# Reordering the halves of the first MLP over three blocks, and taking the first expert pairs' weight splits off GpSimd, in a fused attention–MLP–MoE kernel

## Chip, cores and metric

One NeuronCore of a Trainium2 chip runs the whole program in one launch. The metric is the device time of that launch in microseconds; a kernel's figure is the median of its runs. A chance or a verdict "within 0.2%" means within about 2.2 us.

## What is computed

Three stages follow one another, all in float32. Windowed attention (4 sequences of 768 tokens, 8 heads of 64, chunks of 32 queries that see 16 keys to the left, 8 to the right and 8 memory keys) gives 3072 rows of 512. A dense MLP and then a mixture of 8 experts follow:

```
x = attention(q, k, v, mem_k, mem_v)                  # 3072 x 512
h = x @ w_in                                          # 512 x 2048
g = h * tanh(softplus(h))
y = g @ w_out                                         # 2048 x 512
logits = normalise(y) @ normalise(expert_emb).T / tau
e, p = argmax(logits), softmax(logits)[argmax]
out = p * (relu(y @ w1[e]) @ w2[e])                   # w1[e] 512 x 1024, w2[e] 1024 x 512
```

To keep float32 accuracy each operand of the large products is split into a high and a low part of TensorE's float32 format, and three products are taken: high by high, high by low, low by high.

## The kernel before

**Attention** is cut into 48 sub-units of 64 queries, six to a block of 384 tokens, eight blocks. A sub-unit takes transposes of q and k (`T`), scores (`S`), a softmax on VectorE and ScalarE whose division `norm` (line 453) runs on VectorE or GpSimd, the transposes of the probabilities (`PT`), the product with v (`V`), and the split of the result into `xt`, the block's MLP input (1.5 MB, high and low parts). There are two `xt` buffers.

**The first MLP** has 128 steps. Step s works on one block j and one slice f of 128 of the 2048 hidden units. On TensorE it has `H`, twelve matmuls into `p_h` (line 539), and `Y`, nine matmuls into three accumulators `p_y` (line 585). Between them ScalarE and VectorE evaluate the activation: tanh, square, exp (ScalarE), `m` (line 558), square (line 562, ScalarE), `rr` (line 565), `g` (line 568), `gh` and `gl` (line 576). `p_h` has two buffers, so `H` of step s needs the `g` of step s-2, which is the last reader of its buffer. The accumulators have one buffer each.

The first time that a slice of w_in or w_out is used its 32 pieces must have been loaded (`raw`) and split (`sign`, `high`, `low`, `hi`, `lo`: lines 286 to 316, most of it on VectorE). So the program's front has three streams on VectorE at once: attention, pieces of weights, and the activation. To spread the pieces, before runs the slices of block 0 in two halves: (block 0, slices 0–7), (block 1, slices 0–15), (block 0, slices 8–15), then blocks 2 to 7 in full. The partial y of block 0's first half is evacuated (`out0`), stored in DRAM (`y_p`) and added later.

**Routing** computes the logits of each tile of 128 tokens as the MLP ends it, and then, in two groups (21 tiles, last 3 tiles), the expert of each token and its place: a chain of some dozens of small VectorE operations per group (lines 796 to 1035).

**The experts** run in units of 256 tokens of one expert (pairs) or 128 (singles). The first three pairs, u = 0, 1, 2, come from group 1 alone, and lie at the end of the MLP and beside the routing of group 2. Each pair gathers two tiles of rows (`xg`, an indirect DMA issued by GpSimd), transposes them (`xT`), and loads eight 512 KB chunks of w1 and w2 (`eraw`). Each chunk is split: `ehi` is a copy (ScalarE or VectorE, line 246 is the copy helper) and `elo` a subtraction (VectorE or GpSimd, line 1163). TensorE then runs `eH`, matmuls into `p_h` (line 1191), the relu halves `hh` follow on VectorE (lines 1202, 1208), and `eY`, matmuls into `p_y` (line 1281). The result is scattered to the output by GpSimd (`out_dram`).

**What sets the order.** All instructions are ordered by a planner (`Plan.order`). Each job has a rank and a planned duration on each engine that may do it; the planner simulates the engines, gives each job to the engine that ends it first, and emits the jobs in that order. The order of each engine's queue is then fixed; the chip only waits on the semaphores. Operations in the set `PORT` (line 87) are planned as if VectorE and GpSimd could not run them at the same time as GpSimd's own; the small routing operations (`r`, `ids`) are not in that set. A matmul group of another kind behind the last costs `SWITCH` in the plan.

The lines that set the MLP's order, and the engines of the experts' splits:

```
order = ([(0, f) for f in range(HALF)] + [(1, f) for f in range(KFF)] + [(0, f) for f in range(HALF, KFF)]
         + [(j, f) for j in range(2, NBLK) for f in range(KFF)])
put_job(("shi", u, second, c), hi, {A: 947} if j in (0, 2, 4, 5, 7) else {V_: 602}, ...)
put_job(("slo", u, second, c), lo, {G: 2303} if j in (1, 4, 6) else {V_: 1135}, ...)
```

Of the kernel before, what the change touches and what calls it, by code (L numbers as in the profile page):

```python
# [85 lines left out]

PORT = {"sign", "high", "low", "hi", "lo", "rg", "norm", "rn", "m", "rr", "gh", "gl", "yb2", "yb3", "shi", "slo"}


class Plan:  # L90
# [24 lines left out]
    def order(self):  # L115
        end, on, free, todo, waits, tiled, cols, port = {}, {}, {}, {}, {}, False, {}, 0.0
# [79 lines left out]
def attn_moe_moe_kernel(ctx, tc, q, k, v, mem_k, mem_v, w_in, w_out, emb, tau, w1, w2, cst, out, ydbg=None):  # L196
# [71 lines left out]
    def piece(n):  # L268
# [49 lines left out]
        r = 2 * n - 50 if n < 4 else 0.5 * n - (6 if n < NPIECE // 2 else 0)  # L318
# [16 lines left out]
    def attention(u):  # L335
# [3 lines left out]
        R = lambda x: x + (3 * u - 60 if first else 1.4 * u - 16 if u < 2 * SPB else 1.5 * u + 2 if u < 3 * SPB else 8 * u / 3 - 20.4)  # L339
# [148 lines left out]
        job(("T", u), T, {E: 437 if odd else 560}, rank=R(0), after=[("qk", u)], use=[(t, u) for t in qkt] + ([kt] if odd else []),  # L488
# [30 lines left out]
    y_p = dram.tile([BLK, DM], F32, name="y_p")  # L519

    def mlp(s):
        j, f = order[s]
        g, o = divmod(f, WG)
        first = f == 0 or (j, f) == (0, HALF)
        final = f == KFF - 1 or (j, f) == (0, HALF - 1)
        new = j == (0 if f < HALF else 1)
        yh = (j, f // HALF if j == 0 else 0)

# [915 lines left out]
```

## Time and profile before

| | before |
|---|---|
| median of 3 runs | 1094.82 us (1093.49 to 1095.75) |
| the profiled execution | 1091.25 us |
| its span, first to last instruction | 1089.5 us |
| mean granted TensorE clock over the span | 0.989 |
| TensorE busy | 1054.7 us (97%) |
| VectorE busy | 784.4 us (72%) |
| ScalarE busy | 685.1 us (63%) |
| GpSimd busy | 187.6 us (17%) |

The profile is one execution, followed by instruction. [...] On a timeline an instruction's duration reaches a little into the next one's, so the cost of one in a full queue is the spacing of the starts.

### The profile page before, as it was taken

The page shows a single profiled execution, that of the slowest core. Times are in us where ns is not written, and L with a number is a line of the kernel's source. Part 1 is how long each engine was busy: PE and PEld are TensorE (multiplying, and loading weights), DVE is VectorE, ACT ScalarE, POOL GpSimd, SP SyncE. Part 2 cuts the span into 40 slices and gives each one's busy share as a digit, 9 for nine tenths or more (in the row PEclk, how much of TensorE's full clock was granted, in tenths as well). Part 3 has the DMA queues.
Part 4 walks back from the last instruction along what each step waited for, and adds up shares of the span by engine and source line. Part 5 has one row for each costly group of instructions (what it writes and reads, how often), then busy time and mean ns, then how long its engine had stood idle before and what let it go on. Part 6 is the DMA issues. An engine that isn't in the chain of part 4 may idle for free. (4 is left out here: it accounts for less than half of the span.)

```text
span 1089.5 us, 20349 instructions
## 1 busy us (share of the span) xinstructions
PE 1054.7 (97%) x7501; PEld 923.2 (85%) x7501; DVE 784.4 (72%) x1611; ACT 685.1 (63%) x1559; POOL 187.6 (17%) x114
## 2 busy tenths in 40 slices
PE   8898999999999999999999999999989999999996
PEld 6687888888888888888888889888889889998995
DVE  4999996667676576567667566797995558777851
ACT  4787887667777777768777777855424334444441
POOL 0000000000000000000000000014455545665542
PEclk9999999999999999999999999999999999999998
DMA  7954411322112112112112100019349768568200
GB/s 185 285 169 124 138 30 32 77 69 66 28 43 60 37 38 57 35 36 66 37 30 67 25 14 30 1 41 386 145 160 400 254 233 259 200 205 273 86 31 21
DMA packets 154767, 121.81 MB, mean 112 GB/s; under 512 B 98010, under 2 KB 127066, under 8 KB 154660
## 3 DMA queue, kind: packets, MB, share of 16 engines
q1 hardware_dynamic: 150340, 107.06, 32.2%
q0 software_dynamic: 4320, 13.37, 3.4%
q8 instruction: 61, 1.00, 0.4%
q14 instruction: 46, 0.38, 0.1%
HBM read 115.43 MB, written 14.16 MB: 119 GB/s over the span
## 5 line engine op out<-in xcount | busy, mean ns | idle before, releaser
L539 PE MATMUL p_h<-xt,win_h 128*128 128x384 f32 x1024 | 271.8, 347 | 6.0 <-DVE rn L568 5.9
L539 PEld LDWEIGHTS p_h<-xt,win_h 128*128 128x128 f32 x1024 | 182.4, 189 | 14.8 <-DVE rn L568 5.8
L539 PE MATMUL p_h<-xt,win_l 128*128 128x384 f32 x512 | 173.5, 339 | 0.4 <-DVE win_l L316 0.4
L585 PE MATMUL p_y<-wout_h,gh 128*128 128x512 f32 x384 | 155.1, 404 | 0.5 <-ACT gh L246 0.5
L585 PE MATMUL p_y<-wout_h,gl 128*128 128x512 f32 x384 | 152.1, 396 | 0.6 <-DVE gl L576 0.6
L585 PE MATMUL p_y<-wout_l,gh 128*128 128x512 f32 x384 | 151.6, 395 | 0.0
L1281 PE MATMUL p_y<-ehi,hh 128*128 128x512 f32 x432 | 142.1, 398 | 0.4 <-DVE hh L1250 0.4
L246 ACT CAST ehi<-eraw 128x1024 fp32r<-128x1024 f32 x80 | 83.7, 1049 | 90.7 <-PE p_y L1281 54.7
L1163 DVE TENSOR_TENSOR elo<-eraw,ehi 128x1024 fp32r<-128x1024 f32 x80 | 113.8, 1428 | 34.9 <-ACT ehi L246 34.7
L1163 POOL TENSOR_TENSOR elo<-eraw,ehi 128x1024 fp32r<-128x1024 f32 x48 | 119.4, 2488 | 110.0 <-ACT ehi L246 53.7
L1191 PE MATMUL p_h<-xs,ehi 128*128 128x256 f32 x704 | 131.4, 288 | 5.9 <-DVE hh L1208 2.2
L558 DVE SCALAR_TENSOR_TENSOR m<-sq,rn 128x384 f32<-128x384 f32 x128 | 71.0, 555 | 84.1 <-ACT rn L236 83.4
L1191 PEld LDWEIGHTS p_h<-xs,ehi 128*128 128x128 f32 x704 | 111.9, 193 | 9.0 <-ACT ehi L246 3.3
L543 ACT ACTIVATE sq<-p_h 128x384 f32<-128x384 f32 x128 | 61.8, 483 | 69.2 <-PE p_h L539 69.2
L562 ACT ACTIVATE m<-m,c 128x384 f32<-128x384 f32 x128 | 78.7, 615 | 39.5 <-DVE m L558 38.8
L1191 PE MATMUL p_h<-xs,elo 128*128 128x256 f32 x352 | 100.8, 286 | 1.0 <-DVE elo L1163 1.0
L539 PEld LDWEIGHTS p_h<-xt,win_l 128*128 128x128 f32 x512 | 96.7, 189 | 0.8 <-DVE win_l L316 0.8
L1281 PEld LDWEIGHTS p_y<-ehi,hh 128*128 128x128 f32 x432 | 81.2, 188 | 18.8 <-DVE hh L1250 1.3
L585 PEld LDWEIGHTS p_y<-wout_h,gl 128*128 128x128 f32 x384 | 72.3, 188 | 18.4 <-DVE gl L576 1.0
L565 DVE SCALAR_TENSOR_TENSOR rn<-m,rn 128x384 f32<-128x384 f32 x128 | 71.4, 558 | 20.7 <-ACT m L562 20.0
L1281 PE MATMUL p_y<-elo,hh 128*128 128x512 f32 x216 | 85.2, 394 | 0.0
L585 PEld LDWEIGHTS p_y<-wout_h,gh 128*128 128x128 f32 x384 | 72.4, 189 | 13.6 <-ACT gh L246 0.7
(261 smaller groups left out, 1884.1 us busy)
## 6 DMA issues: line engine op xcount, KB each, us to landing
eraw<-in_moe_w_dram SPq DMA_DIRECT2D x128, 512.0 KB
raw<-in_moe_w_in_dram SPq DMA_DIRECT2D x16, 512.0 KB
raw<-in_moe_w_out_dram SPq DMA_DIRECT2D x16, 512.0 KB
y_d<-ysb SPq DMA_DIRECT2D x24, 256.0 KB
qn<-in_q_dram SPq DMA_DIRECT2D x43, 128.0 KB
kn<-in_k_dram SPq DMA_DIRECT2D x35, 128.0 KB
vn<-in_v_dram SPq DMA_DIRECT2D x20, 176.0 KB
vn<-in_v_dram SPq DMA_DIRECT2D x20, 128.0 KB
```

The source lines that it names most:

```text
L246: (nc.scalar.copy if e == A else nc.vector.tensor_copy)(out, src)
L539: nc.tensor.matmul(p, w, xt[j][:, a, kk, :], start=(n == 0), stop=(n == len(ops) - 1))
L543: nc.scalar.activation(t, tl["h", s], AF.Tanh, scale=0.5)
L558: nc.vector.scalar_tensor_tensor(t, tl["sq", s], 4.0, tl["rn", s], ALU.add, ALU.mult)
L562: nc.scalar.activation(t, t, AF.Square, bias=c15)
L565: nc.vector.scalar_tensor_tensor(tl["rn", s], tl["m", s], 0.75, tl["rn", s], ALU.add, ALU.mult)
L585: nc.tensor.matmul(yp[yh][t], x[:, c], w[g][:, o, :], start=(first and n == 0), stop=(final and n == 2))
L1163: engs[e].tensor_sub(tl["elo", j], raw[b, second, c], tl["ehi", j].bitcast(F32))
L1191: nc.tensor.matmul(p[:, o, :], w[:, kk, s], v[:, kk, :], start=(kk == 0 and m == 0), stop=(kk == KDM - 1 and m == 2))
L1281: nc.tensor.matmul(tl["yy", u][a], v[:, kk, s], w[:, k, :], start=(kk == 0 and m == 0), stop=(kk == KEF - 1 and m == 2))
```

## The change

It has three parts.

1. **MLP order** (`LEAVE = 2`). The first halves of three blocks come first, then their second halves: (block 0, slices 0–7), (block 1, 0–7), (block 2, 0–15), (block 1, 8–15), (block 0, 8–15), then blocks 3 to 7. The second half of the weights is first used at step 24 instead of 16, and its pieces' rank is moved by 5 steps. The attention of blocks 1, 2 and 3 gets other ranks. Three blocks are now under way with two `xt` buffers, so block 0's `xt` is stored in DRAM (`x_p`) after step 7 and read back after step 31 by a DMA on GpSimd's queue; `V` of unit 12, the first writer of block 2's `xt`, takes the buffer that the store frees. Block 1's partial y is now stored and added too, as block 0's was.
2. **Splits of the first three pairs.** All `ehi` of u < 3 go to ScalarE, and all `elo` to VectorE. Per pair that moves three `elo` from GpSimd to VectorE and three `ehi` from VectorE to ScalarE.
3. **Planner.** `r` and `ids` join `PORT`, the switch cost depends on the two kinds of matmul (`between`), a few planned durations change, and gathers are kept in order.

```diff
+LEAVE = 2
+DENSE = {"mm_h", "mm_y", "H", "Y"}
+def between(a, b):
+    if a in DENSE:
+        return 92 if b in ("T", "S", "yL") else 0
+    if b in DENSE:
+        return 0 if a is None else 20 if a in ("PT", "yT", "xT", "hT") else 90
+    return 93 if a in ("PT", "yT") and b in ("T", "S") else 0
-PORT = {"sign", "high", "low", "hi", "lo", "rg", "norm", "rn", "m", "rr", "gh", "gl", "yb2", "yb3", "shi", "slo"}
+PORT = {"sign", "high", "low", "hi", "lo", "rg", "norm", "rn", "m", "rr", "gh", "gl", "yb2", "yb3", "shi", "slo", "r", "ids"}
...
-        r = 2 * n - 50 if n < 4 else 0.5 * n - (6 if n < NPIECE // 2 else 0)
+        r = 2 * n - 50 if n < 4 else 0.5 * n - 6 if n < NPIECE // 2 else 0.5 * n + 5
...
-        R = lambda x: x + (3 * u - 60 if first else 1.4 * u - 16 if u < 2 * SPB else 1.5 * u + 2 if u < 3 * SPB else 8 * u / 3 - 20.4)
+        R = lambda x: x + (3 * u - 60 if first else 1.4 * u - 16 if u < (LEAVE + 1) * SPB else 2 * o + 32 if j == LEAVE + 1 else 8 * u / 3 - 20.4)
...
-    order = ([(0, f) for f in range(HALF)] + [(1, f) for f in range(KFF)] + [(0, f) for f in range(HALF, KFF)]
-             + [(j, f) for j in range(2, NBLK) for f in range(KFF)])
+    order = ([(j, f) for j in range(LEAVE) for f in range(HALF)] + [(LEAVE, f) for f in range(KFF)]
+             + [(j, f) for j in reversed(range(LEAVE)) for f in range(HALF, KFF)]
+             + [(j, f) for j in range(LEAVE + 1, NBLK) for f in range(KFF)])
...
+    def x_away():
+        def store(e):
+            nc.sync.dma_start(out=x_p.bitcast(F32), in_=flat_x(xt[0]).bitcast(F32))
+        def load(e):
+            xt[0] = xp.tile([128, 2, KDM, BLK], F32R, tag="xt", name="xt")
+            nc.gpsimd.dma_start(out=flat_x(xt[0]), in_=x_p)
+        s0, s1 = at[0, HALF - 1], at[LEAVE, KFF - 1]
+        plan.dma(("xstore",), store, dict(SP=470), 3 * 2 ** 19, s0, [("mm_h", s0)], use=[("xt", 0)])
+        plan.dma(("xload",), load, dict(Pool=1100), 3 * 2 ** 19, s1, [("mm_h", s1), ("xstore",)], get=[("xt", ("xt", 0, 1))])
...
-            put_job(("shi", u, second, c), hi, {A: 947} if j in (0, 2, 4, 5, 7) else {V_: 602}, rk, [("ld", u, second, c)], [(f"w{16 + 2 * j}", h1)], [hr_])
-            put_job(("slo", u, second, c), lo, {G: 2303} if j in (1, 4, 6) else {V_: 1135}, rk, [("shi", u, second, c)], [(f"w{17 + 2 * j}", h2)], [hr_, h1])
+            put_job(("shi", u, second, c), hi, {A: 947} if j in (0, 2, 4, 5, 7) or u < FIRST // 2 else {V_: 602}, rk, [("ld", u, second, c)] + ([("shi", u - 1, second, c)] if u else []), [(f"w{16 + 2 * j}", h1)], [hr_])
+            put_job(("slo", u, second, c), lo, {G: 2303} if j in (1, 4, 6) and u >= FIRST // 2 else {V_: 1135}, rk, [("shi", u, second, c)], [(f"w{17 + 2 * j}", h2)], [hr_, h1])
```

What this does to the queues is shown at three places. Line numbers are those of each kernel: GpSimd's `elo` is line 1163 before and 1197 after, the gathers 1086 and 1119, the scatters 1307 and 1341.

GpSimd's queue from the end of the MLP over the first pairs, before:

```order
L1086 DMA xg<-y_d,gi 128x512 x2
L975 CAST ei<-ef 1x3
L1086 DMA xg<-y_d,gi 128x512 x2
L1163 TENSOR_TENSOR elo<-eraw,ehi 128x1024 x5
L1086 DMA xg<-y_d,gi 128x512 x2
L1163 TENSOR_TENSOR elo<-eraw,ehi 128x1024
L1307 DMA out_dram<-yo,si 3072x512 x2
L1163 TENSOR_TENSOR elo<-eraw,ehi 128x1024 x2
L1086 DMA xg<-y_d,gi 128x512 x2
L975 CAST ei<-ef 1x20
L1163 TENSOR_TENSOR elo<-eraw,ehi 128x1024
```

The same place after:

```order
L1119 DMA xg<-y_d,gi 128x512 x2
L1007 CAST ei<-ef 1x3
L1119 DMA xg<-y_d,gi 128x512 x4
L1341 DMA out_dram<-yo,si 3072x512 x3
L1119 DMA xg<-y_d,gi 128x512 x2
L1007 CAST ei<-ef 1x20
L1341 DMA out_dram<-yo,si 3072x512
L1197 TENSOR_TENSOR elo<-eraw,ehi 128x1024
```

Nine `elo` stand in this stretch before (5, 1, 2 and 1). After, only DMAs and one cast of 20 numbers are left until the pairs of group 2.

VectorE's queue in the routing of group 2, where it first meets the pairs (`rc`, `ra`, `rh`, `rd`, `o` are routing; `hh` is the relu), before:

```order
L867 TENSOR_TENSOR ra<-ra,rh 128x24
L1208 SCALAR_TENSOR_TENSOR hh<-p_h_9281,hh 128x512
L868 TENSOR_REDUCE rc<-ra 128x3
L246 CAST ehi<-eraw 128x1024
L869 CAST rc<-rc 128x3
L1163 TENSOR_TENSOR elo<-eraw,ehi 128x1024
L870 TENSOR_SCALAR rc<-rc 128x3
L1208 SCALAR_TENSOR_TENSOR hh<-p_h_9326,hh 128x512
L871 TENSOR_SCALAR rc<-rc 128x3
L872 CAST rh<-rc 128x3
```

After:

```order
L899 TENSOR_TENSOR ra<-ra,rh 128x24
L1197 TENSOR_TENSOR elo<-eraw,ehi 128x1024
L900 TENSOR_REDUCE rc<-ra 128x3
L1197 TENSOR_TENSOR elo<-eraw,ehi 128x1024
L901 CAST rc<-rc 128x3
L1242 SCALAR_TENSOR_TENSOR hh<-p_h_9338,hh 128x512
L902 TENSOR_SCALAR rc<-rc 128x3
L1197 TENSOR_TENSOR elo<-eraw,ehi 128x1024
L903 TENSOR_SCALAR rc<-rc 128x3
L1197 TENSOR_TENSOR elo<-eraw,ehi 128x1024
L904 CAST rh<-rc 128x3
```

The copies `ehi` have left VectorE, and more subtractions `elo` stand between the small routing operations.

GpSimd's queue from the program's start to the end of the MLP (`win`, `wout` and `raw` are pieces of weights, `pr` is the attention's division), before:

```order
L240 TENSOR_SCALAR win_h<-sp 128x512
L453 TENSOR_TENSOR pr<-pr,sm 128x384 x4
L576 TENSOR_TENSOR gl<-rn,gh 128x384
L1086 DMA xg<-y_d,gi 128x512 x2
```

After:

```order
L466 TENSOR_TENSOR pr<-pr,sm 128x384
L253 TENSOR_SCALAR win_h<-sp 128x512
L253 TENSOR_SCALAR wout_h<-sp 128x512
L466 TENSOR_TENSOR pr<-pr,sm 128x352
L329 TENSOR_TENSOR win_l<-sp,win_h 128x512
L329 TENSOR_TENSOR wout_l<-sp,wout_h 128x512
L253 TENSOR_SCALAR raw<-raw 128x512
L329 TENSOR_TENSOR win_l<-sp,win_h 128x512
L466 TENSOR_TENSOR pr<-pr,sm 128x384
L543 DMA xt<-x_p 128x3072
L1119 DMA xg<-y_d,gi 128x512 x2
```

Nine elementwise operations now stand ahead of the reading back of `x_p`; before, five stood in the same stretch of the program, and one more at its end.

## Rows read from the trace of the kernel before

**Rows 1.** The page's first part: busy us, share of the span, instructions.

```profile
PE 1054.7 (97%) x7501; PEld 923.2 (85%) x7501; DVE 784.4 (72%) x1611; ACT 685.1 (63%) x1559; POOL 187.6 (17%) x114
```

**Rows 2.** Stretches (start:end, length, busy us and instructions by engine, PEclk, DMA share, GB/s).

```profile
50.00:100.00 50.00, 45.25 (x342) 37.10 (x341) 49.58 (x110) 42.51 (x111) 1.09 (x1) 0.92 0.58 163
100.00:150.00 50.00, 47.48 (x270) 40.51 (x269) 48.43 (x99) 42.11 (x92) 0.00 (x0) 0.98 0.36 113
...
200.00:250.00 50.00, 48.91 (x463) 41.92 (x460) 35.31 (x85) 34.12 (x101) 2.48 (x3) 1.00 0.31 76
...
850.00:1050.00 200.00, 199.59 (x1308) 181.26 (x1308) 141.99 (x148) 88.66 (x113) 111.99 (x65) 1.00 0.59 198
```

**Rows 3.** The same by 10 us where the first expert pairs and group 2's routing lie.

```profile
750.00:760.00 10.00, 9.96 (x69) 9.57 (x69) 8.79 (x19) 4.39 (x5) 5.86 (x3) 0.83 1.06 401
...
800.00:810.00 10.00, 8.57 (x57) 8.40 (x58) 9.96 (x29) 2.25 (x3) 6.03 (x5) 0.83 0.57 163
```

**Rows 4.** TensorE's waits, 690 to 1089 us: who waited for whom, us, times, longest.

```profile
PE p_h L1191 <- DVE hh L1208: 2.2, 1, 2.2
PE p_h L1191 <- DVE rb L806: 1.7, 1, 1.7
PE p_h L539 <- DVE rn L568: 1.2, 1, 1.2
PE p_h L1191 <- DVE xs L1144: 1.0, 1, 1.0
PE p_h L1191 <- DVE elo L1163: 1.0, 1, 1.0
PE p_h L1191 <- ACT ehi L246: 0.8, 1, 0.8
```

**Rows 5.** VectorE's timeline, routing of group 2: start, us, instruction [idle before].

```profile
744.73 2.36 DVE L1163 TENSOR_TENSOR elo<-eraw,ehi 128x1024 fp32r<-128x1024 f32 x2 [2.06 <-ACT ehi L246]
...
762.79 2.33 DVE L871 TENSOR_SCALAR rc<-rc 128x3 int32<-128x3 int32 x1
765.03 0.16 DVE L872 CAST rh<-rc 128x3 bf16<-128x3 int32 x1
...
793.33 1.21 DVE L1163 TENSOR_TENSOR elo<-eraw,ehi 128x1024 fp32r<-128x1024 f32 x1
...
794.54 0.67 DVE L246 CAST ehi<-eraw 128x1024 fp32r<-128x1024 f32 x1
...
803.46 4.30 DVE L1008 TENSOR_TENSOR rhs<-rhs,rb 128x96 bf16<-128x96 bf16 x12
```

**Rows 6.** GpSimd's timeline in the same stretch.

```profile
750.28 4.72 POOL L1163 TENSOR_TENSOR elo<-eraw,ehi 128x1024 fp32r<-128x1024 f32 x2 [7.43 <-DVE lg L681]
...
762.71 2.39 POOL L1163 TENSOR_TENSOR elo<-eraw,ehi 128x1024 fp32r<-128x1024 f32 x1 [0.46 <-ACT ehi L246]
...
803.55 2.40 POOL L1163 TENSOR_TENSOR elo<-eraw,ehi 128x1024 fp32r<-128x1024 f32 x1 [0.63 <-DVE rb L806]
```

**Rows 7.** ScalarE's `ehi`, by line (instruction, count, busy us, mean ns).

```profile
L246 ACT CAST ehi<-eraw 128x1024 fp32r<-128x1024 f32 x80 | 83.7, 1049 | 90.7 <-PE p_y L1281 54.7
```

**Rows 8.** Stretches of 10 us in the front, one of them and the sum.

```profile
sum 120.00, PE 109.49 PEld 92.67 DVE 117.89 ACT 101.05 POOL 1.09; mean PE 9.12 PEld 7.72 DVE 9.82 ACT 8.42 POOL 0.09
```

**Rows 9.** TensorE's waits, 40 to 300 us.

```profile
PE p_h L539 <- DVE rn L568: 4.7, 5, 2.0
```

**Rows 10.** GpSimd's timeline in the front.

```profile
20.68 0.86 POOL L240 TENSOR_SCALAR win_h<-sp 128x512 fp32r<-128x512 f32 x1 [20.22 <-DVE sp L298]
73.88 1.09 POOL L453 TENSOR_TENSOR pr<-pr,sm 128x384 f32<-128x384 f32 x1 [52.34 <-ACT m L562]
...
247.44 0.83 POOL L453 TENSOR_TENSOR pr<-pr,sm 128x384 f32<-128x384 f32 x1 [26.10 <-ACT xt L246]
```

**Rows 11.** VectorE's timeline beside two of these.

```profile
74.19 1.18 DVE L565 SCALAR_TENSOR_TENSOR rn<-m,rn 128x384 f32<-128x384 f32 x1
...
247.77 0.54 DVE L568 SCALAR_TENSOR_TENSOR rn<-rn,p_h 128x384 f32<-128x384 f32 x1
```

More of the change, by code (lines that the diff above doesn't have):

```diff
@@ L115, in order @@
     def order(self):
-        end, on, free, todo, waits, tiled, cols, port = {}, {}, {}, {}, {}, False, {}, 0.0
+        end, on, free, todo, waits, tiled, last, cols, port = {}, {}, {}, {}, {}, False, None, {}, 0.0
         shared = lambda k, e: e == "Pool" and k[0] not in ("gather", "scatter", "issue", "experts") or e == "DVE" and k[0] in PORT
@@ L158, in order @@
                 t = max(t, t0)
-                if tiled > j["tiled"]:
-                    t += SWITCH
-                tiled = j["tiled"]
+                t += between(last, k[0])
+                last, tiled = k[0], j["tiled"]
                 d = self.stream(cols, t, d, SHARE.get(k[0], 1)) - t
@@ L487, in attention @@
         kt = ("kT", pair)
[L488 removed]
+        job(("T", u), T, {E: 560 if odd else 630}, rank=R(0), after=[("qk", u)], use=[(t, u) for t in qkt] + ([kt] if odd else []),
             get=[("a", t1), ("a", t2), ("qT", ("qT", u))] + ([] if odd else [(ktt, kt)]))
@@ L523, in mlp @@
         g, o = divmod(f, WG)
[L524 to L527, printed above, removed]
+        first = f == 0 or j < LEAVE and f == HALF
+        final = f == KFF - 1 or j < LEAVE and f == HALF - 1
+        new = j == (0 if f < HALF else LEAVE)
+        yh = (j, f // HALF if j < LEAVE else 0)
+        X = ("xt", 0, 1) if j == 0 and f >= HALF else ("xt", j)
         htag = "a" if j == NBLK - 1 and f % 3 == 2 else "h"
@@ L610, in rows @@
         j, t = divmod(i, TPB)
-        yh = (j, 1 if j == 0 else 0)
-        half = slice(t * 128, (t + 1) * 128)
+        yh = (j, 1 if j < LEAVE else 0)
+        half = slice(i * 128, (i + 1) * 128)
         def out0(e):
             tl["y0", i] = att.tile([128, DM], F32, tag=tag0, bufs=dict(kT=1, pT=2)[tag0], name="y0")
-            scale(e, tl["y0", i], yp[0, 0][t], 8.0)
+            scale(e, tl["y0", i], yp[j, 0][t], 8.0)
         def store0(e):
@@ L1091, in unit @@
         for a in range(nt):
+            gathers.append(("issue", "gather", u, a))
             put_job(("gather", u, a), gather(a), {G: 1038}, base - 4,
-                    [("places", g)] + [("ystore", i) for i in range(T1 if g == 1 else NTILE)], [("vn", ("xg", u, a))], dma=2 ** 18)
+                    [("places", g)] + gathers[-2:-1] + [("ystore", i) for i in range(T1 if g == 1 else NTILE)], [("vn", ("xg", u, a))], dma=2 ** 18)
         def load(second, c):
```

44 lines of the change are left out of this document (26 added, 18 removed).

## Prediction

> **What bounds the kernel now.** I read the busy times first: TensorE works 1054.7 of 1089.5 us [rows 1], so at most some 35 us can go without less work, and what matters is where TensorE stands still. The table of stretches puts that in four places [rows 2]: 50 to 100 us (4.75 us idle, and a granted clock of 0.92), 100 to 150 (2.52 us, 0.98), 200 to 250 (1.09 us), and the first expert pairs at 700 to 850. From 850 to 1050 TensorE is busy 199.59 of 200 us, so a gain made earlier is not given back there; the tail after 1050 is not touched by the change.
>
> In the front VectorE is the bound: it works 117.89 of the 120 us from 40 to 160 [rows 8], and TensorE's waits there name its activation step `g` (4.7 us in five waits) [rows 9]. That is the stretch in which attention, weight pieces and activation share VectorE.
>
> In the expert stretch the waits of TensorE are 2.2 (for `hh`), 1.7, 1.2, 1.0, 1.0 and 0.8 us, 7.9 us in all, four of the six on VectorE's routing or relu work and one on its `elo` [rows 4]. Twice the granted clock is 0.83 there, at 750 to 760 and 800 to 810, after such waits [rows 3]: a stretch of 10 us at 0.83 loses (1 − 0.83) × 10 = 1.7 us of work each, 3.4 us. Together that is 11.3 us: the ceiling of what the second part of the change can give.
>
> Why VectorE is late there is on two timelines read side by side. A routing step on 128x3 numbers takes 0.16 us at 765.03, but the one at 762.79 takes 2.33 us and ends at 765.12; GpSimd's `elo` of 762.71 took 2.39 us and ended at 765.10 [rows 5, 6]. The twelve small products at 803.46 take 4.30 us beside the `elo` of 803.55 [rows 5, 6]. There are eight such stretched instructions between 751 and 808; each less what its kind takes alone gives 0.8, 2.1, 2.2, 2.2, 2.2, 1.8, 2.0 and 2.3 us, about 15.7 us of VectorE's time lost beside nine `elo`.
>
> **The change, part by part.** *Splits of the first pairs.* It removes nine `elo` from GpSimd and with them the 15.7 us of stretching. It adds nine `elo` to VectorE, whose spacing is 1.14 us (793.33 to 794.47, the 1.21 us less the overlap) [rows 5]: +10.3 us. It takes nine `ehi` from VectorE at 0.60 us spacing (0.67 on the row) [rows 5]: −5.4 us. VectorE's balance is −15.7 + 10.3 − 5.4 = −10.8 us between about 740 and 808, where it is at 9.96 of 10 us in 800 to 810 [rows 3]. ScalarE takes nine copies of 1.05 us [rows 7]: 9.4 us, in stretches where it is busy 4.39 and 2.25 of 10 us [rows 3]; I put them at nothing, covered by that idle time, and if the cover is gone they are the rival below.
>
> What TensorE gets of the 10.8 us goes wait by wait. The 2.2 (`hh`), 1.7 and 1.0 us (`rb`, `xs`) come behind stretched instructions and should go: 4.9 us. The other three, 1.2, 0.8 and 1.0 us, belong to the first pair's start, when chunks arrive and are split and only one `elo` stands on GpSimd; I take a third of their 3.0 us, 1.0. Of the clock I take the whole second loss, 1.7, and most of the first, 1.4, which lies after these start waits. That is 9.0 us. Bounds: 3 us, if only the wait for `hh` and a little clock go, and 11.3 us. I lean to the upper end because VectorE's relief exceeds the sum of the waits that hang on it. What is late next is the chunks' landing: the DMA engines are full at 750 to 760 (401 GB/s) [rows 3], and those loads start no earlier for the first pairs.
>
> *Order of the MLP.* Pieces of the second half may come eight steps later, but attention of blocks 1 and 2 comes earlier instead. I added up the instructions in front of step 22's `H` in each order, each kind at its mean spacing. VectorE has 13.5 us more ahead of it than before (more score additions, maxima, x splits and copies; four fewer piece subtractions), TensorE 13.0 us more. Before, VectorE was 1.8 us ahead of TensorE at that point; by these sums it now binds and TensorE has lost 1.3 us less than it had. So the front stays bound by VectorE and the half order mostly exchanges one kind of work for another: −1.3 us. The idle 1.09 us at 200 to 250 [rows 2], where attention of block 3 and block 0's return lay, I halve: −0.5. The bounds of the front's own gain are 0 and 5 us, the latter if half of the 8.4 us idle in the three stretches and some of the clock's loss go.
>
> The order's price has three terms. Block 0's `xt` is stored, 1.5 MB; at the 401 GB/s that full DMA engines reached [rows 3] that is 3.9 us, at the 163 GB/s of 50 to 100 us [rows 2] 9.6 us. `V` of unit 12 must wait for it and stands some 10 us of TensorE's work after step 7: nothing, or up to about 3 us with what is queued ahead of the store; VectorE, the bound, has other work meanwhile, so a wait under 5 us costs nothing. Behind the store on SP's queue stand loads of q, k, v and pieces, which have no users for several steps. The reading back has eight steps of 4.2 us for the same transfer: nothing. Block 1's partial y adds three evictions, stores and loads, beside TensorE's work: nothing; they fall after VectorE's full stretch.
>
> GpSimd's elementwise work is the third term. Nine operations now stand ahead of the reading back, where two were at work before 200 us. Three divisions at 0.83, three copies-with-scale at 0.86 [rows 10] and three subtractions, half as long as an `elo` (1.2 us, an estimate from the 2.39 of [rows 6]), make 8.7 us, against 0.86 + 1.09 [rows 10] before: 6.7 us more. What that costs VectorE is not one number: beside the division of 73.88 (1.09 us) the step at 74.19 took 1.18 us, 0.63 longer than the 0.55 of its kind, and beside that of 247.44 nothing was longer [rows 10, 11]. The ends are 0 and 6.7 × 0.63 / 1.09 = 3.9 us; I take the middle, +2.0.
>
> [...]
>
> *Planner.* The new costs and `PORT` entries move instructions but add none. I cost them at nothing; the sums above are made from the resulting orders.
>
> **The sum**, against the profiled 1091.25 us: −9.0 − 1.3 − 0.5 + 2.0 = −8.8; 1082.5. That execution lies 3.6 us under the median of the runs shown, and the median is what is forecast: 1094.82 − 8.8 = 1086.0 us.
>
> **The rivals.**
>
> *The front gains as well.* If the added GpSimd work stretches nothing and the front's gain is its upper 5 us, with an expert gain of 9 to 10, the sum is −14 to −15: 1080. For it: VectorE is the front's bound and some of its work has gone to GpSimd. Against it: the work moved in ahead of step 22 weighs as much as what moved out.
>
> [...]
>
> *The expert stretch is bound by its loads.* Then the start waits and the first clock loss remain and only about 3 us go: 1094.8 − 3 − 0.5, about 1091. For it: the DMA engines are full at 750 to 760. Against it: the waits name VectorE, not a DMA.
>
> *Nothing reaches the end.* The stretches go, but as many `elo` now stand ahead of each routing step and relu, so that the chain to the places and to `hh` is no earlier: 1094.8. The order after does show two `elo` more between such steps.
>
> *Slower: VectorE waits for ScalarE.* Each of the moved chunks now needs a ScalarE copy before VectorE's `elo`, and behind that `elo` on VectorE's queue stand the routing steps and `hh`. The row at 744.73 shows such a wait, 2.06 us for an `ehi` [rows 5]. Nine of these are 18.5 us; with −10.8 that is +7.7 on a full VectorE, and −0.5 from the front: 1102. It is no gain from a mean wait of 10.8 / 9 = 1.2 us on, and slower by over 0.2% from about 1.5 us on. For it: ScalarE works in order and the copies queue behind relu halves and x copies. Against it: ScalarE is idle over half of the stretch, and most chunks landed early.
>
> **How the numbers follow.** Forecast 0.50 (1082.5 to 1089.5); the front gains as well 0.12; the port is held 0.08; bound by loads 0.13; nothing reaches the end 0.07; slower 0.10. A difference within 0.2%, about 2.2 us, is what a measurement here can't tell from none. Faster by more: 0.50 + 0.12 + 0.08 + 0.10 of the loads' case = 0.80. Within: the rest of the loads' case and nearly all of "nothing", 0.09. Slower: 0.11. The range 1079.5 to 1092.5 holds the forecast, the port, most of the front's and the loads' cases: 0.80.
>
> **What would show it.** Between 740 and 800 no routing step of VectorE over 1 us, GpSimd without `elo`, TensorE's waits for `hh`, `rb` and `xs` gone, and the clock at 1.00 in the second of the two stretches: right on the pairs. VectorE at over 97% from 40 to 160, now with instructions stretched beside GpSimd's nine, and TensorE's loss by step 22 within 2 us of before: right on the front. A wait of TensorE of over 5 us at `V` of unit 12, or waits of VectorE for `ehi` above 1.2 us in the mean, would make the prediction wrong; so would the last pair's `eY` ending no more than 5 us earlier than before when counted from the last MLP step.

## The result and the profile after

| | before | after |
|---|---|---|
| median, measured together (4 runs each) | 1095.28 us (1093.49 to 1098.51) | 1080.14 us (1078.09 to 1083.69) |
| ratio, 95% interval | | 0.9862 (0.9827 to 0.9897) |
| the profiled execution | 1091.25 us | 1080.64 us |
| its span | 1089.5 us | 1078.8 us |

The change is 15.1 us faster; 1086.0 had been forecast, and the range 1079.5 to 1092.5 holds the time. The two profiled executions lie 10.6 us apart: before's is 4.0 us under its median, after's 0.5 us over. The traces explain the 10.6.

After's busy times, as in [rows 1] (us, share, instructions):

```profile
PE 1050.8 (97%) x7499; PEld 920.4 (85%) x7499; DVE 776.7 (72%) x1605; ACT 694.1 (64%) x1574; POOL 170.1 (16%) x109
```

After's stretches, columns as in [rows 2] (start:end, length, busy of PE, PEld, DVE, ACT, POOL, granted clock as a share of the full one, DMA share, GB/s):

```profile
0.00:50.00 50.00, 42.91 (x490) 34.40 (x490) 36.73 (x87) 30.97 (x106) 1.02 (x5) 1.00 0.84 228
50.00:100.00 50.00, 47.98 (x405) 39.75 (x406) 49.32 (x115) 41.88 (x121) 4.90 (x4) 0.93 0.68 193
100.00:150.00 50.00, 49.89 (x377) 42.52 (x377) 49.60 (x112) 42.32 (x110) 3.26 (x3) 1.00 0.52 150
150.00:200.00 50.00, 47.09 (x267) 41.00 (x266) 39.12 (x101) 39.02 (x91) 1.20 (x1) 1.00 0.14 39
200.00:250.00 50.00, 50.00 (x306) 44.68 (x305) 31.08 (x64) 37.97 (x84) 0.76 (x1) 1.00 0.21 69
...
750.00:800.00 50.00, 50.00 (x346) 45.31 (x345) 47.77 (x157) 28.93 (x39) 11.12 (x9) 1.00 0.49 178
800.00:850.00 50.00, 49.73 (x340) 44.92 (x340) 36.72 (x37) 19.52 (x27) 29.88 (x15) 1.00 1.04 383
850.00:1050.00 200.00, 196.72 (x1276) 177.75 (x1275) 141.15 (x146) 86.92 (x112) 107.30 (x63) 1.00 0.56 182
```

Against [rows 2]: TensorE works 2.7 and 2.4 us more in the two stretches from 50 to 150, and 750 to 850 is almost without a gap. Two places are worse: 150 to 200 has 2.9 us idle where before had none, and 850 to 1050 lost 3.3 us where before lost 0.4. The 2.9 us are three waits: 1.5 for ScalarE's copy `kT` (157.82), 0.8 for `g` (162.56) and 0.6 for a small VectorE step (174.94). TensorE's waits late in the program, as in [rows 4] (690 to 1080 us):

```profile
PE p_y L1315 <- DVE hh L1284: 3.3, 3, 1.2
PE p_yT L674 <- ACT ysb L249: 1.2, 1, 1.2
PE p_y L614 <- DVE gh L259: 0.5, 1, 0.5
PE p_lg L701 <- DVE yt L259: 0.4, 1, 0.4
PE p_h L1225 <- DVE xs L1178: 0.3, 1, 0.3
```

The six waits of [rows 4] are gone from the first pairs: the three on the activation and the chunks at their start have given way to those in the three middle rows (for `ysb`, `gh` and `yt`, 2.1 us), and the 0.3 us for `xs` belong to u = 4. The 3.3 us in the first row lie behind the pairs, in the singles; before has 0.4 us in two waits there, below the rows shown in [rows 4].

**Where the time went.** TensorE does the same work in both kernels, so its lead over before can be read at equal points of the work: the start of the last `H` but one (719.89 before, 714.00 after), the end of `eY` of u = 2 (827.2 and 813.0) and of u = 4 (875.3 and 861.5), and the last matmul's end (1079.3 and 1068.6). The differences of these leads give what each stretch won, 5.9, 8.3, −0.4 and −3.1 us: the front 5.9, the first three pairs 8.3, and 3.5 given back after them. This table is used for all kernels below.

### The profile page after: what moved, and what is told of

The parts are those of the page before. It is cut to its first block, busy times and chain, and to the rows that moved or that the text cites. A ratio compares the mean times of both kernels' runs of the same rounds, so it can differ in the third digit from the quotient of the medians.

```text
span 1078.8 us, 20397 instructions
## 1 busy us (share of the span) xinstructions
PE 1050.8 (97%) x7499; PEld 920.4 (85%) x7499; DVE 776.7 (72%) x1605; ACT 694.1 (64%) x1574; POOL 170.1 (16%) x109
## 3 DMA queue, kind: packets, MB, share of 16 engines
q1 hardware_dynamic: 151348, 110.21, 33.5%
## 5 line engine op out<-in xcount | busy, mean ns | idle before, releaser
L1197 DVE TENSOR_TENSOR elo<-eraw,ehi 128x1024 fp32r<-128x1024 f32 x89 | 133.4, 1507 | 40.8 <-ACT ehi L259 39.0
L259 ACT CAST ehi<-eraw 128x1024 fp32r<-128x1024 f32 x89 | 92.8, 1048 | 100.5 <-PE p_y L1315 51.4
L1119 POOL DMA_INDIRECT xg<-y_d,gi x27 | 29.7, 1100 | 556.1 <-DVE si L1067 507.5
L1197 POOL TENSOR_TENSOR elo<-eraw,ehi 128x1024 fp32r<-128x1024 f32 x39 | 95.0, 2437 | 82.4 <-ACT ehi L259 47.5
```

The source lines that it names most:

```text
L259: (nc.scalar.copy if e == A else nc.vector.tensor_copy)(out, src)
L1119: nc.gpsimd.indirect_dma_start(out=tl["xg", u, a], out_offset=None, in_=y_d[0:T1 * 128, :] if g == 1 else y_d[:, :], in_offset=bass.Indire ...
L1197: engs[e].tensor_sub(tl["elo", j], raw[b, second, c], tl["ehi", j].bitcast(F32))
```

## The experiments

Ratios are to before in the same series, with 95% intervals; the four series had medians of before of 1092.51, 1094.18, 1092.52 and 1091.66 us. After was not measured again in them: its ratio is that of the result above, from four runs of each kernel, and has the widest interval. The names of the parts are those of the diff above: 1 MLP order, 2 splits, 3 planner.

**Each part alone, and each left out.** `splits_only` is before with part 2, `order_only` with part 1, `planner_only` with part 3; `no_splits`, `no_order` and `no_planner` are after without one. Their edits are the lines shown in the diff, put into before or taken back from after; the first and the last as samples:

```diff
 # splits_only, on before
-{A: 947} if j in (0, 2, 4, 5, 7) else {V_: 602}
+{A: 947} if j in (0, 2, 4, 5, 7) or u < FIRST // 2 else {V_: 602}
-{G: 2303} if j in (1, 4, 6) else {V_: 1135}
+{G: 2303} if j in (1, 4, 6) and u >= FIRST // 2 else {V_: 1135}
 # no_planner, on after
-                t += between(last, k[0])
+                if tiled > j["tiled"]:
+                    t += SWITCH
-"shi", "slo", "r", "ids"}
+"shi", "slo"}
```

Expected of `splits_only`: 

> The kernel before with the second part of the change alone: for the first three pairs every ehi on ScalarE and every elo on VectorE; MLP order and planner as before. If the nine GpSimd subtractions cost the pairs' stretch what the two traces show (the lead of the changed kernel grows from 4.8 us at the last MLP step to 14.1 at the third pair's first matmul, so 9.3 there), this run has 1095 - 9 = 1086 us, and no routing step of VectorE over 1 us between 740 and 800. If it is the planner's new entries that clear the stretch, and the splits only move work, it is within 3 us of before.

Expected of `order_only`: 

> The kernel before with the first part of the change alone: first halves of three blocks, then second halves, attention ranks with it, block 0's x stored and read back; splits and planner as before. If the order of the MLP alone makes the front's gain, TensorE reaches the last MLP step 4 to 5 us earlier and the run has 1095 - 5 = 1090 us. If my sum for the front was right (1.3 + 0.5 less 2.0 for GpSimd's added work, about nothing) and the gain of the front comes from the planner's new durations and switch costs, it is 1094 to 1096.

Expected of `planner_only`: 

> The kernel before with the third part alone: r and ids in the set that is planned as excluding GpSimd, the switch cost by kinds, the changed planned durations, gathers in order. Charged at nothing in the prediction: 1093 to 1097 us. If the planner's entries are what clears the routing of stretched steps, 1086 to 1090.

Expected of `no_planner`: 

> The changed kernel without the third part: MLP order and splits as changed, planner as before. The parts alone gave ratios of 0.9914 (splits), 0.9921 (order) and 1.0002 (planner). If splits and order work in different places and add up, 0.9836: about 1075 us, faster than the changed kernel. If the changed kernel's smaller total (0.9862) is the ceiling of what TensorE can be given, whatever the planner, 1078 to 1081.

Expected of `no_splits`: 

> The changed kernel with the first three pairs' splits as before: order and planner changed. The planner alone won 4 to 5 us in the front and lost about 8 in the pairs' stretch, where nine elo were still on GpSimd. If that is what it does with GpSimd's elo, this run repeats it: about 1093 + 0 to -4, 1089 to 1094. If the order and the planner add up without it, 1084.

Expected of `no_order`: 

> The changed kernel with the MLP order of before: splits and planner changed. If order and planner both win the same idle time in the front (each alone reaches the last MLP step earlier than before, the order by about 8 us and the planner by about 5), this run keeps the planner's share and the splits' 9: 1080 to 1083. If only the order wins in the front, 1084 to 1087.

Measured, with the gains by stretch from each trace (us, minus is a loss against before):

| parts | kernel | ratio | front | u = 0–2 | u = 3, 4 | rest |
|---|---|---|---|---|---|---|
| 2 | `splits_only` | 0.9914 (0.9894–0.9933) | 0.4 | 8.3 | 0.1 | −0.7 |
| 1 | `order_only` | 0.9921 (0.9903–0.9938) | 8.0 | −0.3 | 0.0 | −0.4 |
| 3 | `planner_only` | 1.0002 (0.9990–1.0013) | 6.3 | 3.0 | −11.2 | −1.1 |
| 1, 2 | `no_planner` | 0.9838 (0.9822–0.9855) | 8.3 | 8.4 | 0.0 | −4.1 |
| 1, 3 | `no_splits` | 1.0003 (0.9991–1.0016) | 6.6 | 4.1 | −12.7 | −0.1 |
| 2, 3 | `no_order` | 0.9865 (0.9846–0.9884) | 4.8 | 8.3 | 0.1 | −3.8 |
| 1, 2, 3 | after | 0.9862 (0.9827–0.9897) | 5.9 | 8.3 | −0.4 | −3.1 |

Three things follow. Every kernel with the splits has won 8.3 to 8.4 us at the first pairs. Alone, the splits account for all of it; beside part 3 they do not, since 3.0 to 4.1 us are won there without them, and what they then add most is that the 11 to 13 us at u = 3 and 4 are not lost. The order alone gives 8.0 us in the front, which no sum of mine had; but beside part 3 it adds nothing (0.9865 without it, 0.9862 with it), since the planner's new costs win 4.8 to 6.3 us in the front by themselves, and the two gains do not add up (5.9 and 6.6 us with both). And part 3 is not neutral: with `elo` on GpSimd it loses 11 to 13 us at u = 3 and 4, as much as it wins before. Parts 1 and 2 add up as independent gains would: 0.9914 × 0.9921 = 0.9836, measured 0.9838.

In `order_only` the stretches show the front's gain: 45.25 and 47.48 became 46.41 and 50.00 us, and the clock 0.97 and 1.00 where it was 0.92 and 0.98 [rows 2].

```profile
50.00:100.00 50.00, 46.41 (x403) 38.22 (x404) 49.37 (x115) 43.29 (x127) 2.77 (x3) 0.97 0.68 191
100.00:150.00 50.00, 50.00 (x380) 42.96 (x379) 49.50 (x110) 42.97 (x112) 4.17 (x3) 1.00 0.52 154
```

In `planner_only` the loss at u = 4 stands on the timelines of VectorE, GpSimd and TensorE:

```profile
831.47 2.37 DVE L1176 TENSOR_TENSOR elo<-eraw,ehi 128x1024 fp32r<-128x1024 f32 x1
833.76 0.69 DVE L257 CAST ehi<-eraw 128x1024 fp32r<-128x1024 f32 x1
834.37 3.79 DVE L1176 TENSOR_TENSOR elo<-eraw,ehi 128x1024 fp32r<-128x1024 f32 x1
838.08 0.68 DVE L1221 SCALAR_TENSOR_TENSOR hh<-p_h,hh 128x512 fp32r<-128x512 f32 x1
838.68 1.27 DVE L1157 TENSOR_TENSOR xs<-p_xT,xs 128x512 fp32r<-128x512 f32 x2
```

```profile
830.38 2.38 POOL L1176 TENSOR_TENSOR elo<-eraw,ehi 128x1024 fp32r<-128x1024 f32 x1 [6.21 <-issue]
...
834.71 2.35 POOL L1176 TENSOR_TENSOR elo<-eraw,ehi 128x1024 fp32r<-128x1024 f32 x1
```

```profile
840.01 0.58 PE L1204 MATMUL p_h<-xs,ehi 128*128 128x256 f32 x1 [5.01 <-DVE xs L1157]
```

Two of VectorE's `elo` take 2.37 and 3.79 us instead of 1.21 [rows 5] beside GpSimd's two, the `xs` queued behind them is 3.7 us late, and TensorE waits 5.0 us for it. That is part of the 11.2 us: in the same stretch TensorE also waits 1.9 us for a GpSimd `elo` itself and 0.7 us twice, and the clock falls once (3.4 us). The group's places, the last step of routing, come at 804.45 us (798.70 before) although the front was 6.3 us earlier. Which of part 3's edits puts these pieces beside one another was not tried; that `r` and `ids` now yield to GpSimd in the plan fits the later routing, and is argued only.

**Is it GpSimd's work that delayed VectorE?** `dummies` gave after GpSimd work again at the first pairs, nine subtractions into a scratch tile, cut into eight pieces each:

```diff
+for n in range(8):
+    z = slice(128 * n, 128 * n + 128)
+    nc.gpsimd.tensor_sub(dummy, raw[b, second, c][:, z], tl["ehi", j][:, z].bitcast(F32))
```

> The changed kernel with nine GpSimd subtractions put back in the first three pairs (each in eight pieces of 128 columns), which read the same chunk and its high part, and write a scratch tile that nobody reads; the order on every other engine is that of the changed kernel, instruction for instruction, and the output is the same. If GpSimd's subtractions hold up VectorE's own instructions, routing steps between 740 and 800 are stretched again, VectorE loses up to the 21 us that nine of them last, and the time is 1080 + 5 to 10 = 1085 to 1090 us. If the stretching before came from something else (the order, waits on data), no step is stretched and the time stays within 2 us of 1080.

It took 1.0040 (1.0024–1.0055), but tells little: the 72 pieces took 51 us, and ScalarE's next `ehi` had to wait for these readers of the old one:

```profile
762.39 1.04 ACT L260 CAST ehi<-eraw 128x1024 fp32r<-128x1024 f32 x1 [7.19 <-POOL dummy L1210]
```

That is another wait than the one in question. VectorE's order is after's, so its instructions can be compared one by one: from 735 to 810 us 34 of them are longer, each by 0.2 to 0.3 us, 8.4 us in all, but what of the lost time is due to them and what to the wait cannot be told apart. `pool_back` mended it: nine additions of zero in full size, in place on a chunk whose `elo` is done, so that neither `ehi` nor `elo` waits for them directly.

```diff
+zero = const.tile([128, 1], F32, name="zero")
+nc.gpsimd.tensor_tensor(t, t, zero.to_broadcast([128, 1024]), ALU.add)
```

> The changed kernel with nine GpSimd instructions of the size of an elo put back in the first three pairs: each adds a zero in place to a chunk that VectorE has already split, so nobody but the load of the pair after next waits for it; every other engine has the changed kernel's order, and the output is the same. It repeats the run with eight small pieces without that run's flaw, that ScalarE's next ehi waited for the GpSimd readers. If GpSimd's instruction holds up VectorE's, routing steps or relu halves of over 1 us return between 740 and 800, VectorE loses some 10 us and the time is 5 to 9 us over the changed kernel, 1085 to 1089. If the losses came by data waits and order alone, it stays within 2 us of the changed kernel, 1078 to 1082.

1.0099 (1.0080–1.0117), and again not usable: its first `H` already came at 45.6 us, against 39.25 in after, long before the additions. The new 4-byte tile had moved all buffers behind it; that is taken up below. `pool_back2` takes the zero from a column of the constants, and moves nothing:

```diff
-zero.to_broadcast([128, 1024])
+cf[:, 128 + NK:129 + NK].to_broadcast([128, 1024])
```

> The run that puts nine GpSimd instructions of an elo's size back into the first three pairs, again, without the flaw of the first one: there a 4-byte tile for the zero moved all buffers behind it, and even the front's loads came some 6 us later. Now the zero is a column of the constants, no buffer moves, and the order on every other engine is that of the changed kernel. The front should then be the changed kernel's (last MLP step at 720 to 722 us). If GpSimd's instruction holds up VectorE's: routing steps of over 1 us again, and 1080 + 5 to 9 = 1085 to 1089 us. If the first run's loss was the moved buffers alone, 1078 to 1082.

0.9981 (0.9966–0.9995), where after is 0.9862: the nine additions cost about 1.2%, some 13 us in the median (5 to 9 had been expected) and 7.5 in the profile. The order of instructions on TensorE, VectorE, ScalarE and SP is after's. By stretch, against before: front 6.5, u = 0–2 2.0, u = 3 and 4 −6.0, rest 0.6; so 6.3 of the 8.3 us won at the first pairs are gone. The timelines of VectorE, GpSimd and TensorE:

```profile
749.96 1.19 DVE L899 TENSOR_TENSOR ra<-ra,rh 128x24 f32<-128x24 f32 x1
...
752.29 2.82 DVE L1197 TENSOR_TENSOR elo<-eraw,ehi 128x1024 fp32r<-128x1024 f32 x1
...
759.32 1.87 DVE L905 CAST rc<-rc 128x3 f32<-128x3 int32 x1
```

```profile
748.29 5.74 POOL L1208 TENSOR_TENSOR eraw<-eraw,cf 128x1024 f32<-128x1024 f32 x2 [7.08 <-DVE elo L1197]
758.27 5.13 POOL L1208 TENSOR_TENSOR eraw<-eraw,cf 128x1024 f32<-128x1024 f32 x2 [4.24 <-DVE rh L904]
```

```profile
765.96 0.79 PE L1320 MATMUL p_y<-elo,hh 128*128 128x512 f32 x1 [4.07 <-DVE elo L1197]
```

The step at 749.96 ends at 751.15, halfway through GpSimd's pair of additions, of which the first ends at 751.10; that at 759.32 ends at 761.19, GpSimd's first addition there at 761.17. The same cast takes 0.17 us in after (757.97). Eight of VectorE's instructions between 735 and 810 us are longer than in after, by 0.5 to 1.7 us, 10.0 us in all. After 759.32 VectorE runs without a gap, and TensorE waits 4.1 us for the `elo` at its end. So GpSimd's elementwise work delays VectorE's steps, and this reaches TensorE: shown for the first pairs. The loss at u = 3 and 4 is another: an addition also holds its chunk's buffer longer, and the loads come later (128 GB/s from 800 to 810, 371 in after), so that ScalarE waits for a chunk:

```profile
811.54 1.05 ACT L259 CAST ehi<-eraw 128x1024 fp32r<-128x1024 f32 x1 [10.46 <-DMA eraw<-in_moe_w_dram]
```

The 13 us are therefore not the price of the delay alone.

**What a moved buffer costs.** `shift4` is after with an unused constant of 4 bytes:

```diff
+pad = const.tile([128, 1], F32, name="pad")
+nc.vector.memset(pad, 0.0)
```

> The changed kernel with one more constant tile of 4 bytes per partition, which is set once and never read, so that all buffers behind it lie 4 bytes higher. If the place of the buffers slows the loads (in the first run with it the DMA engines were at least as busy in the first 50 us and moved 176 to 204 GB/s where the changed kernel had 208 to 288), the first MLP step starts some 6 us later and the run ends 8 to 15 us later, 1088 to 1095. If that run's loss came from its GpSimd work alone, 1078 to 1082.

0.9960 (0.9944–0.9976), 1% above after, though no instruction but one memset is new. Its first two stretches against after's above:

```profile
0.00:50.00 50.00, 43.18 (x441) 33.83 (x442) 29.39 (x74) 24.34 (x87) 1.03 (x5) 0.93 0.93 194
50.00:100.00 50.00, 40.40 (x330) 33.42 (x329) 44.37 (x98) 37.81 (x106) 2.22 (x3) 0.86 0.81 171
```

The DMA engines are busier (0.93 and 0.81; 0.84 and 0.68) and move less (194 and 171 GB/s; 228 and 193). All of the loss lies in the front, which is 7.8 us behind before where after is 5.9 ahead.

**A version without GpSimd's `elo`.** The new waits for `hh` in after come behind a stretched `elo` in the singles, here the first of three (VectorE, GpSimd, TensorE):

```profile
891.16 4.06 DVE L1197 TENSOR_TENSOR elo<-eraw,ehi 128x1024 fp32r<-128x1024 f32 x1 [0.99 <-ACT ehi L259]
...
895.75 0.68 DVE L1284 TENSOR_TENSOR hh<-p_hT,hh 128x512 fp32r<-128x512 f32 x1
```

```profile
891.72 2.42 POOL L1197 TENSOR_TENSOR elo<-eraw,ehi 128x1024 fp32r<-128x1024 f32 x1
```

```profile
896.48 0.73 PE L1315 MATMUL p_y<-ehi,hh 128*128 128x512 f32 x2 [1.12 <-DVE hh L1284]
```

So `np_all` is `no_planner` with every `ehi` on ScalarE and every `elo` on VectorE, in all units:

```diff
-{A: 947} if j in (0, 2, 4, 5, 7) or u < FIRST // 2 else {V_: 602}
+{A: 947} if j in (0, 2, 4, 5, 7) or True else {V_: 602}
-{G: 2303} if j in (1, 4, 6) and u >= FIRST // 2 else {V_: 1135}
+{G: 2303} if j in (1, 4, 6) and False else {V_: 1135}
```

> The fastest version so far (MLP order and splits changed, planner as before, 1077 us) with the same splits for all pairs and singles: every ehi on ScalarE, every elo on VectorE, none on GpSimd. In that version TensorE waits 4.1 us in the singles for VectorE's hh, which stands behind an elo stretched beside GpSimd's. If that is the lock again, the waits go: 1073 to 1075. If VectorE and ScalarE now have too much in the singles (8 elo of 1.14 us and the rest make some 11.5 of 13.2 us), new waits take their place: 1077 to 1085.

What the runs show of "the lock" are VectorE's `elo` of 4.06 us beside GpSimd's of 2.42 here and of 2.82 us beside an addition in `pool_back2`, where an undisturbed one takes 1.22.

1072.66 us (1071.70 to 1074.04), 0.9821 (0.9802–0.9840): the fastest of all, below both kernels. Its stretches: front 8.4, u = 0–2 9.2, u = 3 and 4 0.1, rest +0.9. The waits for `hh` are gone, and TensorE is busy throughout the singles:

```profile
850.00:1050.00 200.00, 200.00 (x1316) 182.42 (x1315) 148.79 (x160) 112.75 (x135) 33.93 (x32) 1.00 0.54 179
```

VectorE does more there (148.79 against 141.15 us in after) and is still not the bound. The rest of the units gained 5.0 us over `no_planner` (0.9 against −4.1).

`np_all_480` adds a constant of 480 bytes to it, to see whether another place for the buffers is better or worse:

```diff
+pad = const.tile([128, 120], F32, name="pad")
```

> The fastest version so far (MLP order changed, planner as before, no elo on GpSimd anywhere; ratio 0.9821) with 480 bytes per partition more in the constants, so that all buffers behind them lie 480 bytes higher instead of 4 as in the run that lost 10 us. If what slowed that run was a start at an odd multiple of 4 bytes, a shift by a multiple of 32 costs nothing: 0.980 to 0.984. If any move of the buffers from where they are costs, 0.99. If the buffers of before lie at a bad place and a round one is better, under 0.979.

0.9932 (0.9910–0.9953): the loss of `shift4` again, 1.1%, and again in the front (0.0 us won where `np_all` has 8.4).

## Why the prediction held, and where it did not

**The pairs: right in mechanism and nearly in size, the size in part by luck.** Forecast 9.0 us, measured 8.3 by the splits alone (`splits_only`), and 8.3 in after. The signs came as written: in after no single routing step between 740 and 800 takes 1 us, GpSimd's first `elo` comes at 806.28, the waits for `hh`, `rb` and `xs` are gone from the pairs, and the clock is 1.00 at 800 to 810. The terms of the sum can be read at equal work, from the last `H` but one to the end of `eY` of u = 2, in before, `splits_only` and after (columns as in [rows 2]):

```profile
719.89:827.20 107.31, 98.82 (x643) 87.36 (x642) 92.78 (x234) 47.88 (x75) 45.43 (x27) 0.97 0.63 224
719.47:818.47 99.00, 95.49 (x643) 85.38 (x642) 81.73 (x234) 54.06 (x81) 17.73 (x17) 0.98 0.64 224
714.00:813.01 99.01, 97.02 (x643) 86.35 (x642) 80.73 (x237) 52.46 (x76) 21.37 (x17) 0.97 0.63 224
```

With the splits alone VectorE works 11.1 us less, where I had 10.8. TensorE's idle time falls from 8.5 to 3.5, so 5.0 us came of it where I had taken 5.9: the 4.9 us of the waits for `hh`, `rb` and `xs` went, and of the three waits at the first pair's start nothing did, where I had taken a third of 3.0. They stand in `splits_only` as before:

```profile
PE p_h L1191 <- DVE elo L1163: 1.5, 2, 1.0
PE p_h L539 <- DVE rn L568: 1.2, 1, 1.2
PE p_h L1191 <- ACT ehi L246: 0.8, 1, 0.8
```

(The 1.2 us are the MLP's own last wait for `g`. I had counted it with routing and relu.) Clock: I took 3.1 us, and the splits alone gave the second loss, 1.7; the first still stands, 0.95 and 0.88 in the two stretches from 730 to 750, of which I had taken 1.4. So 6.7 us came from the two columns instead of 9.0. The other 1.6 us of the 8.3 are in neither; part of them lies beside the waits, where matmuls stand further apart and count as busy (the last one before the wait for `hh` in before, at 779.51, counts 0.28 us, where in the full queue the next one starts after 0.12). That the total came within 0.7 us of the forecast is to that extent luck.

In after the start is different again. Three other waits stand there (for `gh`, `ysb` and `yt`), 2.0 us instead of 3.0, and `no_order` has them too while `no_planner` does not: they come with part 3. And the clock falls once, for longer:

```profile
740.00:750.00 10.00, 10.00 (x63) 9.96 (x63) 6.91 (x13) 5.30 (x7) 0.00 (x0) 0.66 1.06 401
750.00:760.00 10.00, 10.00 (x60) 8.74 (x59) 9.82 (x21) 9.10 (x15) 0.92 (x1) 1.00 1.07 393
...
800.00:810.00 10.00, 10.00 (x52) 8.38 (x52) 3.83 (x5) 2.75 (x5) 3.56 (x2) 1.00 1.06 371
```

One loss of 0.34 × 10 = 3.4 us stands where two of 1.7 stood [rows 3]. TensorE had been idle 1.54 us of 730 to 740.

**The front: wrong.** Forecast −1.3 − 0.5 + 2.0, a loss of 0.2; measured a gain of 5.9 (8.0 for part 1 alone). Up to the last `H` but one TensorE is idle 15.8 us before and 12.3 after, 3.5 less; the granted clock costs it 5.1 and 3.4 us, 1.7 less (an estimate: each stretch of 10 us times 1 minus its clock); 0.7 is in neither. Three terms failed.

The first is what I drew from VectorE's balance up to step 22. The balance itself was right: my sums gave VectorE 13.5 us and TensorE 13.0 us more ahead of that `H`, and the traces have 11.6 and 11.1 more (from the start to that `H`, before and after):

```profile
0.00:165.79 165.79, 151.67 (x1180) 126.37 (x1181) 148.85 (x347) 126.62 (x341) 2.15 (x6) 0.97 0.55 153
0.00:174.94 174.94, 162.81 (x1409) 135.14 (x1409) 160.41 (x379) 137.01 (x393) 10.38 (x13) 0.98 0.62 174
```

TensorE's idle time up to there fell from 14.1 to 12.1 us, 2.0 where I had 1.3, and behind it by another 1.5 where I had 0.5. I read the balance as "the front stays bound by VectorE" and went to the low end. VectorE did stay full (118.89 of 120 us from 40 to 160, against 117.89 in [rows 8]), but TensorE did 112.91 us of work beside it instead of 109.49, and its waits for `g` fell from 4.7 us in five to 0.8 in one [rows 9]. Between 40 and 160 us it ran 528 matmuls of attention (`T`, `S`, `PT`, `V`) instead of 312, and 377 of `H` and `Y` instead of 415. A full engine is the bound only for the work that hangs on it: the half order puts more TensorE work that needs no activation beside the same VectorE time. That this is why the waits for `g` went is argued from these counts; the parts of the new order (halves, ranks of pieces and of attention) were not tried one by one.

The second is the clock, which I had only in the upper bound. Before, it falls twice in the front, to 0.66 at 50 to 60 us and to 0.93 and 0.90 from 90 to 110, behind the longest of the waits for `g` (2.0 us, at 97.31). In after that wait is gone, and the clock falls once, to 0.66 at 50 to 60.

The third is GpSimd's nine operations in the front, charged at +2.0. From 40 to 160 us five of VectorE's instructions are longer beside them (by 0.64, 0.42 and three times 0.1 us), and one by 0.63 at 173.65, where VectorE is no longer full; before had one by 0.63 [rows 11]. That is +0.7 to 1.3 us of VectorE's time, inside the ends 0 and 3.9 but under the middle. VectorE's and GpSimd's rows at two of these places in after:

```profile
79.99 0.68 DVE L329 TENSOR_TENSOR win_l<-sp,win_h 128x512 fp32r<-128x512 f32 x1
80.59 0.58 DVE L459 TENSOR_SCALAR sm<-sm 128x4 f32<-128x4 f32 x1
...
98.91 1.19 DVE L587 SCALAR_TENSOR_TENSOR m<-sq,rn 128x384 f32<-128x384 f32 x1
```

```profile
79.74 1.40 POOL L253 TENSOR_SCALAR wout_h<-sp 128x512 fp32r<-128x512 f32 x1 [10.92 <-DVE sp L311]
...
98.40 1.28 POOL L329 TENSOR_TENSOR win_l<-sp,win_h 128x512 fp32r<-128x512 f32 x1 [15.02 <-ACT win_h L259]
```

The step at 80.59 ends at 81.17, with GpSimd's at 81.14; but that GpSimd copy took 1.40 us where one of its form took 0.86 [rows 10], while VectorE's `win_l` beside it took its usual 0.68. Another of its form took 1.44 (67.38). So in these two places it was GpSimd's copy that took longer. The step at 98.91 took 1.19 us, 0.64 more than its kind, and ends at 100.10, 0.42 us behind GpSimd's subtraction (1.28 us, to 99.68). I had put all of the stretching on VectorE's side. The forecast counts "the port is held" with 0.08: no run shows a port, and beside the 6.7 us that GpSimd was to work more in the front, VectorE's instructions were longer by 0.7 to 1.3 us.

No wait of TensorE at `V` of unit 12 shows, so the store of `xt` cost nothing, as said.

**The planner: "nothing" was the wrong step.** It was forecast at zero because it adds no instructions. Alone it is zero (1.0002), but as +9.3 and −12.3; in company it wins nothing on top of the order: 0.9862 with it stands against 0.9838 without (the intervals overlap), and in the traces most of that is the front, 5.9 against 8.3.

**The rest of the units: not foreseen.** I wrote that a gain made earlier is not given back from 850 on, because TensorE was full there. It gave back 3.1 us: the singles have the same `elo` on GpSimd, and where TensorE arrives earlier VectorE's stretched `elo` stands in front of `hh`. Before has only 0.4 us of such waits. In `np_all`, without GpSimd's `elo`, waits and loss are gone. It takes the last `ehi` off VectorE as well, so that not all of its 5.0 us need be GpSimd's.

**The rivals, and luck.** The measured 1080.14 is that of "the front gains as well" (1080, chance 0.12). Two of its conditions held, little stretching beside the added GpSimd work and a front that gave 5 us and more, the third nearly (8.3 us at the pairs, where it had 9 to 10). But its sum of 14 to 15 us is not what the traces show: 3.5 us were given back, and the profiled executions differ by 10.6, near the 8.8 of the forecast's sum. The other 4.5 us come from before's profiled execution, which lies that much lower against its median than after's does. I had taken that distance as 3.6 us and added it to both kernels alike. The likeliest case's own range, 1082.5 to 1089.5, missed; that the whole range held the time, and that the traced sum is 1.8 us off, is in part luck, since a front that won 6.1 us more than forecast was set against 3.5 us given back later and 0.7 less at the pairs.

"VectorE waits for ScalarE" did not come, though its waits did, and above the bound that I had set (mean 1.2 us):

```profile
DVE elo L1197 <- ACT ehi L259: 12.9, 7, 3.5
```

12.9 us in seven, 1.8 in the mean (725 to 830 us), and still no loss. Before had 5.0 us in three such waits in this stretch, so 7.9 us are new, less than the 10.8 behind the bound, which I should have set on the added waits. Four of the seven lie between 731 and 745, where VectorE has idle time (6.91 of 10 us busy at 740 to 750), three behind 799 (3.83 of 10 at 800 to 810), and none in the stretch between, where it has next to none. A bound on a mean wait says little when the waits and the full stretch lie apart.

## What to carry over

Before moving work to an idle GpSimd, look at what stands beside it on VectorE: an `elo` of 2.4 us there cost VectorE up to as much, and taking it all back was worth 8 us at the first pairs and up to 5 in the later units. Where a planner sets the order, time each part alone and each left out: here the planner's part was worth +9 and −12 us at two places and read as nothing. And when an experiment adds a buffer, first see that the stretches ahead of it are unchanged.

## What the runs showed of the hardware

An unused constant of 4 bytes cost 1% (0.9960 in `shift4`, 0.9862 in after). It moved the later buffers by 32 bytes: in the built programs `qn` starts at 151808 and the lowest of the experts' chunks at 20736 in before and after; in `shift4` and `pool_back` the buffers of q, k, v and of the chunks start 32 bytes further, in `np_all_480` 480, in `dummies` 512. The first three had the slow loads (194, 189 and 189 GB/s in the first 50 us, first `H` at 45.5 to 45.7 us), `dummies` did not (225 GB/s; 41.3 us, against 39.25 in after). For the same 151348 packets the DMA queue's share of 16 engines is 33.5% in after and 35.6% in `shift4`:

```profile
q1 hardware_dynamic: 151348, 110.21, 33.5%
```

```profile
q1 hardware_dynamic: 151348, 110.21, 35.6%
```

With the spans, 0.335 × 16 × 1078.8 / 151348 makes 38.2 ns a packet, and 0.356 × 16 × 1089.6 / 151348 makes 41.0. `np_all` and `np_all_480` give 38.3 and 41.0 in the same way, `dummies` 38.1. By size, the 90624 packets of 256 bytes took 18.2 ns each in after and 18.1 in `dummies`, 21.0 in `shift4` and 20.8 in `np_all_480`; those of 2 KB took 93.9 and 97.7 ns in after and `shift4`. So a packet took longer in the mean with the buffers moved by 32 and by 480 bytes (41.0 ns), and not by 512 (38.1); why, no run here shows.

A small VectorE step with one input was longer beside GpSimd's work, as one with two was: the 128x3 cast above took 1.87 us beside an addition on GpSimd in `pool_back2`, and 0.17 in after; the 128x24 product `ra` of 749.96 took 1.19 us, and 0.17 in after (751.22).
